# One f pair of each token pair by seven block products accumulated in the output's own banks, with double-width operand tiles, two weight slots and scattered due times

## The chip, the core and the metric

The kernel runs on one core of one Trainium2 chip. The metric is the device time of one execution in microseconds (us), the median of several runs. The kernel before takes 2160.39 us (three runs, 2159.62 to 2161.54). A core has five instruction streams that run side by side and wait for each other by semaphores: TensorE (PE, matrix products, with its weight loads PEld), VectorE (DVE), ScalarE (ACT), GpSimd (POOL), and SyncE (SP), which here issues the DMAs. On-chip tiles lie in SBUF; products are summed in eight PSUM banks of 128 x 512 numbers.

## The reference

Inputs are q, k, v of shape (4, 6080, 256), a scalar tau, w_in (256 x 2048) and w_out (2048 x 256), all 32-bit floats.

```python
qn = q / (norm(q, axis=1) + 1e-06);  kn = k / (norm(k, axis=1) + 1e-06)
s = kn.transpose(0, 2, 1) @ qn / tau          # 4 x 256 x 256
a = softmax(s, -1)
x = (v @ a).reshape(24320, 256)
h = x @ w_in                                  # 24320 x 2048
g = where(h >= 1, h, where(h <= -1, 0, (h + 1)**2 / 4))
out = g @ w_out                               # 24320 x 256
```

## The kernel before

The softmax of a batch is small, so the kernel first makes a matrix W = a @ w_in for each of the four batches and then computes h = v @ W, g, and g @ w_out. The last two products are nearly all of the work. Every product is made with three matmuls (`mm3`, line 473): each operand is split into a rounded first part and a rest (`hi` and `lo`), and first x first, first x rest, rest x first are summed. The three matmuls of one block are called a block product here.

A batch's 6080 tokens are cut into six token pairs (five of 2 x 512 tokens, the last of 2 x 480), and the 2048 hidden features into eight f pairs of 2 x 128. A token pair with an f pair is a group; there are 4 x 6 x 8 = 192 of them, numbered g. In each group:

- `h_ops` (line 801) makes the 2 x 2 blocks of h by `strassen` (line 642): seven block products instead of eight, in the banks A, B and Z. The banks serve as accumulators, and between products ScalarE copies a bank (lines 644, 646) and VectorE sums a bank and a copy (lines 649, 653).
- `tile_ops` (line 784) makes g of each of the four blocks: two ScalarE operations (saturate, line 790; square, 792), a VectorE maximum (794), and the split into a first part (796, ScalarE or VectorE, whichever the planner takes) and a rest (798, VectorE).
- `o_ops` (line 819) adds the group's share of the output into four banks, O00, O01, O10 and O11: eight block products. After the eighth f pair ScalarE copies the banks out (line 838) and SP stores them.

Meanwhile the Gram matrix and the softmax of the next batch are made (`gram_chunk`, `square_piece`, `softmax`), and seven sums of v's blocks for the next token pair (`make_V`, with four differences on GpSimd, line 746). The weights of a group (`w`, 896 KB with both parts) are made once a batch, stored in DRAM, and loaded again for each token pair (`load_W`) into one of four slots.

Nothing is run in the order in which it is written. Each operation is recorded with an engine, a planned duration, the buffers it reads and writes, and a due time (16 per group plus an offset). `Order.run` (line 125) then plays the program through: for each engine it takes, of the operations whose inputs are ready and whose pools have a free buffer, the one with the earliest due time, and so writes the engine's order. Pools marked `ordered` hand out buffers in the order in which they were asked for. A planned duration is a line in the number of columns; the planner knows a cost for a table load of ScalarE only as a longer first exponential (line 571), and none for two engines that disturb each other.

Of the kernel before, what the change touches and what calls it, by code (L numbers as in the profile page):

```python
# [58 lines left out]
class Order:  # L59
# [11 lines left out]
    def op(self, eng, dur, fn, r=(), w=(), due=0.0, gates=(), size=0, other=None, slack=0.0):  # L71
# [53 lines left out]
    def run(self):  # L125
# [3 lines left out]
        for o in self.ops:  # L129
            o.count = len(o.deps) + len(o.gates)  # L130
# [18 lines left out]
        while left:  # L149
            pick = None  # L150
            for e, ops in avail.items():
                now = free[e]
                best = None
                for o in ops:
                    t = base[o.n, e]
                    if best is not None and t > now + SOON and t >= best[0][0]:
                        continue
# [11 lines left out]
                    key = (now, o.due, o.n) if t <= now or o.due <= URGENT and t <= now + SOON else (t, o.due, o.n)  # L169
# [10 lines left out]
            for b in o.bufs:  # L180
                if b.ap is None:
# [44 lines left out]
U = 32  # L226
# [17 lines left out]
ET_SLACK = (2.0, 3.0)  # L244

# [10 lines left out]
def channel_attention_moe(ctx: ExitStack, tc: tile.TileContext, kq, kqT, vT, tau, w_in, w_out, outT):  # L256
# [42 lines left out]
    wout = sb("wout", [FP, 2, 2, C], F32R)  # L299

# [16 lines left out]
    u_mem = sb("u_mem", [6 * TB])  # L317
# [7 lines left out]
        "g": Pool([sb("g6", [2, TB], F32R), *[lambda j=j, h=h: slot2(j, h) for j in range(3) for h in range(2)]]),  # L325
        "w": Pool([w_mem[:, i * WSZ:(i + 1) * WSZ].rearrange("p (a j f) -> p a j f", a=2, j=NS) for i in range(4)]),
# [4 lines left out]
        "u": Pool([u_mem[:, i * TB:(i + 1) * TB] for i in range(6)]),  # L331
# [21 lines left out]
    pools["g"].held[1:] = [kq_all] * 6  # L353
# [10 lines left out]
    pools["u"].held[:4] = [u2_all] * 4  # L364
# [10 lines left out]
    def buf(pool):  # L375
        return Buf(pools[pool])
# [615 lines left out]
```

## Time and profile before

| | before |
|---|---|
| median of three timed runs | 2160.39 us (2159.62 to 2161.54) |
| profiled execution, span of its instructions | 2158.3 us |
| TensorE busy | 2147.2 us (99%), 9872 instructions |
| VectorE busy | 1783.1 us (83%) |
| ScalarE busy | 1593.0 us (74%) |
| GpSimd busy | 245.0 us (11%) |
| DMA, mean | 172 GB/s |

A busy time is the length of the span in which the engine ran at least one instruction. The span runs from the first instruction to the end of the last; the timed runs take in what lies around it. In the views, a group of instructions is told by its line, engine, operation and tiles (out<-in, buffer numbers left out), then its count, its busy time and the mean of one in ns, and the idle time of its engine ahead of it with what ended that idle time. Matmuls overlap, so the mean of one is longer than the distance from one to the next.

### The profile page before, as it was taken

How to read it: one execution, taken by the hardware profiler on the slowest of the kernel's cores; microseconds unless marked ns; L12 is line 12 of the kernel's file. 1: busy time of each engine (PE TensorE's matmuls, PEld its weight loads, DVE VectorE, ACT ScalarE, POOL GpSimd, SP SyncE). 2: the span in 40 equal slices, each digit the busy share in tenths (PEclk: the TensorE clock that was granted, in tenths of full speed). 3: DMA queues.
4: the chain of work that ended last, by engine and by line, in shares of the span. 5: the costliest groups of instructions: out<-in, count | busy, mean ns of one | idle time of the engine just before them, and what ended most of it. 6: DMA issues, size and time to landing. Idle time of an engine off the chain costs nothing.

```text
span 2158.3 us, 27952 instructions
## 1 busy us (share of the span) xinstructions
PE 2147.2 (99%) x9872; PEld 1802.1 (83%) x9872; DVE 1783.1 (83%) x2893; ACT 1593.0 (74%) x2818; POOL 245.0 (11%) x260
## 2 busy tenths in 40 slices
PE   9999999999999999999999999999999999999999
PEld 7888888888888888888888888888888888888887
DVE  7898888878798888888879888888787988777776
ACT  6687778777778777776778877777677777777776
POOL 0230020100131000000023000000012300001000
PEclk9999999999999999999999999999999999999999
DMA  9765366545665444544656455454556532332331
GB/s 385 299 225 172 130 205 206 174 164 156 202 222 181 172 158 163 202 156 133 198 174 234 173 183 172 154 192 140 138 201 202 173 124 91 132 126 94 121 120 36
DMA packets 124604, 371.46 MB, mean 172 GB/s; under 512 B 17968, under 2 KB 49584, under 8 KB 121904
## 3 DMA queue, kind: packets, MB, share of 16 engines
q1 hardware_dynamic: 124464, 369.67, 50.1%
q8 instruction: 78, 1.28, 0.2%
q14 instruction: 62, 0.51, 0.1%
HBM read 298.84 MB, written 70.78 MB: 171 GB/s over the span
## 4 chain that ended last, share of the span: by engine, by line
PE 96%; DMA 2%; DVE 1%; ACT 0%; POOL 0%; issue 0%; SPq 0%; ACTq 0%; DVEq 0%; POOLq 0%
PE bank L473 94%; PE bank L875 1%; DMA kq<-kq 1%; DMA raw_mem<-w_out 1%; DMA raw_mem<-vT 0%; DMA outT<-y_mem 0%; DVE mh_mem L891 0%; POOL t L746 0%; DVE u_mem L404 0%; ACT u_mem L790 0%; DVE w_mem L708 0%; ACT u_mem L792 0%; POOL cols L532 0%; DVE v L755 0%; DVE u_mem L401 0%
## 5 line engine op out<-in xcount | busy, mean ns | idle before, releaser
L473 PE MATMUL bank<-x,wout 128*128 128x512 f32 (+1 forms) x3948 | 1013.4, 388 | 0.0
L473 PEld LDWEIGHTS bank<-x,wout 128*128 128x128 f32 x3948 | 739.3, 188 | 147.0
L473 PE MATMUL bank<-v,w_mem 128*128 128x512 f32 (+1 forms) x3264 | 849.3, 388 | 1.1 <-ACT bank L646 0.6
L473 PEld LDWEIGHTS bank<-v,w_mem 128*128 128x128 f32 x3264 | 610.8, 188 | 122.9 <-ACT bank L646 1.2
L790 ACT ACTIVATE u_mem<-bank 128x512 f32<-128x512 f32 (+1 forms) x576 | 341.3, 593 | 252.9 <-PE bank L473 240.4
L794 DVE TENSOR_TENSOR u_mem<-bank,u_mem 128x512 f32<-128x512 f32 (+1 forms) x576 | 390.9, 680 | 131.3 <-ACT u_mem L792 130.2
L792 ACT ACTIVATE u_mem<-u_mem 128x512 f32<-128x512 f32 (+1 forms) x768 | 471.0, 626 | 6.8
L798 DVE TENSOR_TENSOR x<-u_mem,x 128x512 fp32r<-128x512 f32 (+1 forms) x658 | 457.1, 701 | 13.8 <-ACT x L796 8.7
L796 ACT CAST x<-u_mem 128x512 fp32r<-128x512 f32 (+1 forms) x300 | 183.9, 615 | 92.7 <-DVE u_mem L794 91.6
L649 DVE TENSOR_TENSOR bank<-bank,mh_mem 128x512 f32<-128x512 f32 (+1 forms) x198 | 137.2, 693 | 96.8 <-PE bank L473 93.0
L473 PE MATMUL bank<-x,w_mem 128*128 128x512 f32 (+1 forms) x768 | 208.8, 388 | 0.9 <-ACT bank L646 0.9
L473 PE MATMUL bank<-g,wout 128*128 128x512 f32 (+1 forms) x660 | 182.8, 387 | 0.0
L746 POOL TENSOR_TENSOR t<-raw_mem 128x512 f32<-128x512 f32 (+1 forms) x48 | 67.8, 1411 | 925.0 <-DMA raw_mem<-vT 542.7
L653 DVE TENSOR_TENSOR mh_mem<-bank,mh_mem 128x512 f32<-128x512 f32 (+1 forms) x198 | 135.6, 685 | 40.2 <-PE bank L473 35.2
L473 PEld LDWEIGHTS bank<-x,w_mem 128*128 128x128 f32 x768 | 143.6, 188 | 30.0 <-ACT bank L646 1.3
L797 DVE CAST x<-u_mem 128x512 fp32r<-128x512 f32 (+1 forms) x358 | 159.6, 452 | 8.0
L644 ACT COPY mh_mem<-bank 128x512 f32<-128x512 f32 (+1 forms) x198 | 115.3, 582 | 59.4 <-PE bank L473 57.3
L794 DVE TENSOR_TENSOR u_mem<-mh_mem,u_mem 128x512 f32<-128x512 f32 (+1 forms) x192 | 135.6, 706 | 13.6 <-ACT u_mem L792 13.3
L473 PEld LDWEIGHTS bank<-g,wout 128*128 128x128 f32 x660 | 123.7, 188 | 24.5
L646 ACT COPY bank<-bank 128x512 f32<-128x512 f32 (+1 forms) x198 | 113.4, 573 | 33.7 <-PE bank L473 28.0
L746 POOL TENSOR_TENSOR t<-raw_mem,t 128x512 f32<-128x512 f32 (+1 forms) x48 | 66.8, 1392 | 496.3 <-DVE v L755 394.1
L790 ACT ACTIVATE u_mem<-mh_mem 128x512 f32<-128x512 f32 (+1 forms) x192 | 118.9, 619 | 5.1 <-DVE mh_mem L653 3.7
(104 smaller groups left out, 1432.5 us busy)
## 6 DMA issues: line engine op xcount, KB each, us to landing
w_mem<-w_d SPq DMA_DIRECT2D x160, 896.0 KB, 4.6
raw_mem<-kqT SPq DMA_DIRECT2D x60, 512.0 KB, 6.2
w_d<-w_mem SPq DMA_DIRECT2D x32, 896.0 KB, 4.5
raw_mem<-kq SPq DMA_DIRECT2D x51, 512.0 KB, 5.5
kq<-kq SPq DMA_DIRECT2D x20, 1024.0 KB, 9.1
raw_mem<-vT SPq DMA_DIRECT2D x40, 512.0 KB, 6.3
outT<-y_mem SPq DMA_DIRECT2D x80, 256.0 KB, 2.8
win_mem<-wop_d SPq DMA_DIRECT2D x21, 512.0 KB, 5.6
```

Source lines behind the costliest of these rows:

```text
L473: nc.tensor.matmul(out, lhsT=lhs(a), rhs=rhs(c), start=start and m == 0, stop=stop and m == 2, skip_group_check=skip)
L644: op("ACT", act_us(n), lambda: nc.scalar.copy(m5.ap[:, :n], a.ap[:, :n]), r=[a], w=[m5], due=early)
L646: op("ACT", act_us(n), lambda: nc.scalar.copy(a.ap[:, :n], z.ap[:, :n]), r=[z], w=[a], due=early)
L649: op("DVE", dve_us(n), lambda: nc.vector.tensor_tensor(out=bb.ap[:, :n], in0=z.ap[:, :n], in1=m5.ap[:, :n], op=ALU.add), r=[z, m5], w=[bb] ...
L653: op("DVE", dve_us(n), lambda: nc.vector.tensor_tensor(out=h22.ap[:, :n], in0=z.ap[:, :n], in1=m5.ap[:, :n], op=ALU.add), r=[z, m5], w=[h2 ...
L746: op("POOL", pool_us(n), lambda: nc.gpsimd.tensor_tensor(out=tt(x), in0=a(), in1=c(), op=ALU.subtract), r=r, w=[ts[x]], due=due + d, gates ...
L790: op("ACT", act_us(n), lambda: nc.scalar.activation(us(), src(), IDENTITY_SAT240, scale=240.0), r=[h], w=[u], due=d_sat)
L792: op("ACT", act_us(n), lambda: nc.scalar.activation(us(), us(), AF.Square, bias=0.5, scale=1.0 / 480.0), w=[u], due=d_sq)
L794: op("DVE", dve_us(n), lambda: nc.vector.tensor_tensor(out=us(), in0=src(), in1=us(), op=ALU.max), r=[h], w=[u], due=d_max)
L796: op("ACT", act_us(n), lambda: nc.scalar.copy(t.ap[:, 0, :n], us()), r=[u], w=[t], due=d_hi, other=("DVE", dve1_us(n), lambda: nc.vector.t ...
L797: other=("DVE", dve1_us(n), lambda: nc.vector.tensor_copy(t.ap[:, 0, :n], us())) if g >= FIRST else None)
L798: op("DVE", dve_us(n), lambda: nc.vector.tensor_tensor(out=t.ap[:, 1, :n], in0=us(), in1=f32(t.ap[:, 0, :n]), op=ALU.subtract), r=[u], w=[ ...
```

## The change

In token pairs 2 to 6 of each batch (`SPLIT`), the first f pair's part of the output is made by seven block products. Four go into the four output banks directly. Three go into the bank O01 one after the other: after the first direct products ScalarE copies O01 and O11 aside, the bank takes one more product, VectorE adds the copy of O11 and keeps the sum, the bank takes the next product, ScalarE copies it, and then the last product. The other f pairs accumulate as before, and at the end VectorE adds the saved parts to three of the four banks. The operands are four differences of g blocks, made by GpSimd, and four sums of w_out blocks, made once.

Around it: tiles for g and its split hold two blocks each (`u` 5 x 1024, `g` 4 x 2 x 2 x 512 columns); the pool `w` has two slots instead of four; new pools `c` and `c2` hold the differences and copies; offsets of due times stand in two tables; in 30 of 96 stretches of due times a fixed pattern is added to each; the scratch for DMA descriptors is set to 1024. AHEAD is negative, so that the new branch in `run` takes nothing.

```diff
+            seed, width = NUDGE.get(max(0, int(o.due // (G * NUDGE_GROUPS))), (0, 0))
+            if seed and o.due > -100:
+                o.due += width * scatter(o.n, seed)
...
-U = 32
+U = 32.76
...
+SPLIT = ((0, 1, 1, 1, 1, 1), (0, 1, 1, 1, 1, 1), (0, 1, 1, 1, 1, 1), (0, 1, 1, 1, 1, 1))
+WN = 2
+T_STR = {
+    'sat00': 0.31,
...
-        "w": Pool([w_mem[:, i * WSZ:(i + 1) * WSZ].rearrange("p (a j f) -> p a j f", a=2, j=NS) for i in range(4)]),
+        "w": Pool([w_mem[:, i * WSZ:(i + 1) * WSZ].rearrange("p (a j f) -> p a j f", a=2, j=NS) for i in range(WN)], ordered=True),
...
+    def combos(g):
+        b, k, i = groups[g]
+        n = pairs[k][1]
+        d = G * g
+        u0, u1 = gu[g]
+        c2, c = sums[b, k, i] = buf("c2"), buf("c")
+        c2.parts, c.parts = [Buf(ap=()), Buf(ap=())], [Buf(ap=())]
+        for k_, out, o, a, x, c_, y in ((0, c2, 1, u1, 1, u1, 0), (1, u1, 0, u1, 0, u0, 0), (2, c2, 0, u1, 1, u1, 0),
+                                        (3, c, 0, u0, 1, c2, 0)):
+            op("POOL", pool_us(n), lambda out=out, o=o, a=a, x=x, c_=c_, y=y: nc.gpsimd.tensor_tensor(
+                out=half_of(out, o, n), in0=half_of(a, x, n), in1=half_of(c_, y, n), op=ALU.subtract),
+               r=[a.parts[x], c_.parts[y]], w=[out.parts[o]], h=[out, a, c_], due=d + T_STR["sum"][k_])
...
+    def strassen_o(g):
...
+        first = T_STR["direct"]
+        mm(o(0, 1), w_(i, 0, 0), wout_buf[i], gt[g, 0], 0, i == 0, d + first[0])
+        mm(o(1, 0), s_(i, 3), wsum_buf[i], gt[g, 1], 1, i == 0, d + first[1])
+        mm(o(1, 1), s_(i, 0), wsum_buf[i], gt[g, 1], 0, i == 0, d + first[2])
+        mm(o(0, 0), w_(i, 1, 0), wout_buf[i], gt[g, 0], 1, i == 0, d + first[3])
...
+        copy(z, (0, 0))
+        copy(o(1, 1), "m5")
+        late = lambda key, j: [(x, d + e + T_STR["late"] * (j - i)) for x, e in T_STR[key]]
+        t23 = [operand(sums[b, k, j][0], n, (late("hi2", j), late("lo2", j))) for j in range(SPLIT[b][k])]
+        for j in range(SPLIT[b][k]):
+            mm(z, s_(j, 1), wsum_buf[j], t23[j], 0, False, d + T_STR["chain"][0])
+        op("DVE", dve_us(n), lambda: nc.vector.tensor_tensor(out=r[1, 0].ap[:, :n], in0=z.ap[:, :n], in1=r["m5"].ap[:, :n],
+                                                            op=ALU.add), r=[z, r["m5"]], w=[r[1, 0]], due=early)
+        for j in range(SPLIT[b][k]):
+            mm(z, s_(j, 2), wsum_buf[j], t23[j], 1, False, d + T_STR["chain"][1])
+        copy(z, (1, 1))
+        for j in range(SPLIT[b][k]):
+            t = operand(sums[b, k, j][1], n, (late("hi4", j), late("lo4", j)))
+            mm(z, w_(j, 1, 1), wout_buf[j], t, 0, False, d + T_STR["chain"][2])
...
+                    r = sums.get((b, k), {}).get((y, ct))
+                    if r:
+                        op("DVE", dve_us(n), lambda o=o, yb=yb, r=r: nc.vector.tensor_tensor(
+                           out=yb.ap[:, :n], in0=o.ap[:, :n], in1=r.ap[:, :n], op=ALU.add), r=[o, r], w=[yb], due=due)
...
-                softmax(b + 1, d + 8)
+                softmax(b + 1, d + 19.26)
```

Two places of the built order. The first is TensorE's at the first f pair of the third token pair. Banks 0, 1, 6 and 7 are A, B and Z of h; banks 2 to 5 are O00, O01, O10 and O11; `wout` is w_out and `wsum` its sums. Before:

```order
L473 MATMUL bank4_112<-g6_94,wout_77 128x512 x3
L473 MATMUL bank5_113<-x1_703,wout_77 128x512 x3
L473 MATMUL bank7_115<-x3_1040,w_mem_85 128x512 x3
L473 MATMUL bank1_109<-x3_1040,w_mem_85 128x512 x3
L473 MATMUL bank5_113<-g6_94,wout_77 128x512 x3
L473 MATMUL bank7_115<-v0_95,w_mem_85 128x512 x3
L473 MATMUL bank0_108<-v4_99,w_mem_85 128x512 x3
L473 MATMUL bank2_110<-x0_675,wout_77 128x512 x3
L473 MATMUL bank6_114<-v5_100,w_mem_85 128x512 x3
L473 MATMUL bank2_110<-x2_752,wout_77 128x512 x3
L473 MATMUL bank3_111<-x0_675,wout_77 128x512 x3
L473 MATMUL bank3_111<-x2_752,wout_77 128x512 x3
```

and now:

```order
L575 MATMUL bank4_118<-x1_746,wsum_78 128x512 x3
L575 MATMUL bank3_117<-g0_95,wout_77 128x512 x3
L575 MATMUL bank7_121<-x3_1030,w_mem_86 128x512 x3
L575 MATMUL bank5_119<-x1_746,wsum_78 128x512 x3
L575 MATMUL bank2_116<-g0_95,wout_77 128x512 x3
L575 MATMUL bank1_115<-x3_1030,w_mem_86 128x512 x3
L575 MATMUL bank0_114<-v4_100,w_mem_86 128x512 x3
L575 MATMUL bank3_117<-x2_781,wsum_78 128x512 x3
L575 MATMUL bank7_121<-v0_96,w_mem_86 128x512 x3
L575 MATMUL bank6_120<-v5_101,w_mem_86 128x512 x3
L575 MATMUL bank2_116<-x1_746,wout_77 128x512 x3
L575 MATMUL bank3_117<-x2_781,wsum_78 128x512 x3
```

Before, the f pair has two rows for each of the four O banks (the first of bank 4 stands three rows above this piece). Now it has one row for each, and bank 3 takes two more here (with `wsum`) and a third 13 rows further down; the row of bank 2 with x1 belongs to the next f pair.

The second place is ScalarE's at the softmax of batch 2, in the last token pair of batch 1; the same rows stand at the softmax of batches 3 and 4. `sf_mem` holds the scores, so the rows that write it are the two exponentials. Before:

```order
L790 ACTIVATE u_mem_90<-bank7_115 128x512
L571 ACT_TABLE_LOAD
L571 ACTIVATE sf_mem_88,cols0_75<-sf_mem_88,cols0_75 128x256
L792 ACTIVATE u_mem_90<-u_mem_90 128x512
L571 ACTIVATE sf_mem_88,cols0_75<-sf_mem_88,cols0_75 128x256
L644 COPY mh_mem_86<-bank0_108 128x480
L796 CAST x2_752<-u_mem_90 128x512
L646 COPY bank0_108<-bank6_114 128x480
L796 CAST x2_752<-u_mem_90 128x512
L790 ACT_TABLE_LOAD
L790 ACTIVATE u_mem_90<-bank0_108 128x480
L792 ACTIVATE u_mem_90<-u_mem_90 128x480
```

and now (L673 is the exponential, L899 the saturation, L903 the square, L923 the cast):

```order
L673 ACT_TABLE_LOAD
L673 ACTIVATE sf_mem_89,cols0_75<-sf_mem_89,cols0_75 128x256
L899 ACT_TABLE_LOAD
L899 ACTIVATE u_mem_91<-bank0_114 128x480
L673 ACT_TABLE_LOAD
L673 ACTIVATE sf_mem_89,cols0_75<-sf_mem_89,cols0_75 128x256
L903 ACTIVATE u_mem_91<-u_mem_91 128x480
L899 ACT_TABLE_LOAD
L899 ACTIVATE u_mem_91<-mh_mem_87 128x480
L899 ACTIVATE u_mem_91<-bank1_115 128x480
L903 ACTIVATE u_mem_91<-u_mem_91 128x480
L923 CAST x2_781<-u_mem_91 128x480
```

A saturation has moved between the two exponentials, and two more table loads stand with it. Behind this piece follow a square, a saturation, `COPY mh_mem<-bank0`, a square and `COPY bank0<-bank7`; ahead of it stand `COPY bank0<-bank6` and three casts.

## Rows read from the trace of the kernel before

**Rows 1.** The page: busy us, share of the span and instructions of each engine

```profile
PE 2147.2 (99%) x9872; PEld 1802.1 (83%) x9872; DVE 1783.1 (83%) x2893; ACT 1593.0 (74%) x2818; POOL 245.0 (11%) x260
```

**Rows 2.** Windows: stretch, us, busy (instructions) of PE, PEld, DVE, ACT, POOL; PEclk, DMA

```profile
200.00:2150.00 1950.00, 1949.53 (x8951) 1636.33 (x8952) 1614.53 (x2648) 1450.33 (x2586) 209.40 (x215) 1.00 0.48 162
```

**Rows 3.** Waits of PE (us in total, times, longest), then the last on its timeline

```profile
PE bank L875 <- DMA kq<-kq: 3.0, 4, 1.7
PE bank L473 <- ACT bank L646: 1.5, 2, 0.9
...
200.47 0.96 PE L473 MATMUL bank<-x,w_mem 128*128 128x512 f32 x3 [0.91 <-ACT bank L646]
```

**Rows 4.** Timeline of PE: start us, us, instructions; at 170 and at 560 us

```profile
170.15 0.84 PE L473 MATMUL bank<-x,wout 128*128 128x512 f32 x3
170.83 0.84 PE L473 MATMUL bank<-g,wout 128*128 128x512 f32 x3
...
559.93 0.81 PE L473 MATMUL bank<-v,w_mem 128*128 128x480 f32 x3
560.58 1.46 PE L473 MATMUL bank<-x,wout 128*128 128x480 f32 x6
```

**Rows 5.** Groups by line and shape: busy us, mean ns | idle before

```profile
L790 ACT ACTIVATE u_mem<-bank 128x512 f32<-128x512 f32 x480 | 286.4, 597 | 212.2 <-PE bank L473 203.8
L796 ACT CAST x<-u_mem 128x512 fp32r<-128x512 f32 x255 | 157.3, 619 | 69.7 <-DVE u_mem L794 68.5
L798 DVE TENSOR_TENSOR x<-u_mem,x 128x512 fp32r<-128x512 f32 x549 | 385.2, 709 | 11.7 <-ACT x L796 7.6
L649 DVE TENSOR_TENSOR bank<-bank,mh_mem 128x512 f32<-128x512 f32 x166 | 115.9, 698 | 70.1 <-PE bank L473 69.3
L746 POOL TENSOR_TENSOR t<-raw_mem 128x512 f32<-128x512 f32 x40 | 57.4, 1436 | 712.2 <-DMA raw_mem<-vT 497.0 <-DVE mh_mem L653 97.0 <-DVE v L755 91.9
```

**Rows 6.** Timeline of ACT at the softmax of batch 2

```profile
510.06 1.28 ACT L571 ACT_TABLE_LOAD   x1
511.35 0.51 ACT L571 ACTIVATE sf_mem<-sf_mem,cols 128x256 f32<-128x256 f32 x1
511.77 0.18 ACT L571 ACTIVATION_READ_ACCUMULATOR sf_mem<-sf_mem,cols 128x1 f32 x1
...
513.32 0.62 ACT L796 CAST x<-u_mem 128x512 fp32r<-128x512 f32 x1
513.84 0.55 ACT L646 COPY bank<-bank 128x480 f32<-128x480 f32 x1
...
515.75 1.28 ACT L790 ACT_TABLE_LOAD   x1
517.04 0.57 ACT L790 ACTIVATE u_mem<-bank 128x480 f32<-128x480 f32 x1
517.65 0.60 ACT L792 ACTIVATE u_mem<-u_mem 128x480 f32<-128x480 f32 x1
```

**Rows 7.** Tile w_mem: the DMAs that load and store the weights' slots

```profile
DMA to landing us min/median/max: 3.5/4.6/13.5
```

**Rows 8.** SP's timeline from 488 us, and DMA issues there (KB, us to landing)

```profile
488.74 0.37 SPq L556 DMA_DIRECT2D rn_d<-cols  x1
490.39 0.32 SPq L379 DMA_DIRECT2D w_mem<-w_d  x1
...
w_mem<-w_d SPq DMA_DIRECT2D x2, 896.0 KB, 9.4
rn_d<-cols SPq DMA_DIRECT2D x1, 1.0 KB, 9.9
```

**Rows 9.** Timeline of DVE and of POOL at 301 to 305 us

```profile
300.71 0.69 DVE L798 TENSOR_TENSOR x<-u_mem,x 128x512 fp32r<-128x512 f32 x1
302.97 2.39 DVE L798 TENSOR_TENSOR x<-u_mem,x 128x512 fp32r<-128x512 f32 x2
...
303.01 1.80 POOL L746 TENSOR_TENSOR t<-raw_mem 128x512 f32<-128x512 f32 x1 [11.03 <-DVE x L797]
```

More of the change, by code (lines that the diff above doesn't have):

```diff
@@ L51 @@
 SOON = 0.3
+AHEAD, RATE = -21.03, 40.8
 class Op:
@@ L155, in run @@
                     t = base[o.n, e]
-                    if best is not None and t > now + SOON and t >= best[0][0]:
+                    if best is not None and t > now + max(SOON, AHEAD) and t >= best[0][0]:
                         continue
@@ L244, with scatter @@
 ET_SLACK = (2.0, 3.0)
+NUDGE_GROUPS = 2
+NUDGE = {
[4 rows of a table added]
+}
+def scatter(n, seed):
+    x = (n * 2654435761 + seed * 2246822519 + 374761393) & 0xFFFFFFFF
+    x ^= x >> 15
+    x = (x * 2246822519) & 0xFFFFFFFF
+    x ^= x >> 13
+    return x / 2**32 - 0.5
+SPLIT = ((0, 1, 1, 1, 1, 1), (0, 1, 1, 1, 1, 1), (0, 1, 1, 1, 1, 1), (0, 1, 1, 1, 1, 1))
+WN = 2
+T_PLAIN = {
+    'sat00': 6.19,
+    'sq00': 5.81,
+    'max00': 11.17,
+    'sat01': 14.41,
+    'sq01': -6.66,
+    'max01': 14.91,
+    'sat11': 17.12,
+    'sq11': 19.51,
+    'max11': 17.91,
+    'sat10': 19.72,
+    'sq10': 16.46,
+    'max10': 2.66,
+    'sq': 22.46,
+    'hi0': ((0, 14.67), (1, 22.07)),
+    'lo0': ((0, 19.38), (1, 26.54)),
+    'hi1': ((0, 20.12), (1, 21.1)),
+    'lo1': ((0, 19.91), (1, 21.44)),
+    'o': ((34.75, 36.49, 40.21, 37.06), (24.93, 26.82, 30.64, 29.37)),
+}
+T_STR = {
+    'sat00': 0.31,
+    'sq00': -6.27,
+    'max00': 12.71,
+    'sat01': 0.0,
+    'sq01': 9.23,
+    'max01': 36.97,
+    'sat11': 12.74,
+    'sq11': 18.89,
+    'max11': 26.25,
+    'sat10': 29.07,
+    'sq10': 17.32,
+    'max10': 7.81,
+    'sq': 47.08,
+    'hi0': ((0, -2.0), (1, 28.38)),
+    'lo0': ((0, 27.88), (1, 21.87)),
+    'hi1': ((0, 20.4), (1, 22.7)),
+    'lo1': ((0, 5.64), (1, 13.79)),
+    'sum': (30.04, 31.22, 27.0, 22.88),
+    'direct': (21.09, 27.49, 26.88, 27.74),
+    'chain': (30.85, 43.19, 53.35),
+    'hi2': ((0, 25.07), (1, 42.64)),
+    'lo2': ((0, 28.65), (1, 34.17)),
+    'hi4': ((0, 41.98),),
+    'lo4': ((0, 46.16),),
+    'late': -18.42,
+    'early': 5.9,
+}
 HEAD = (2,)
@@ new lines, in strassen_o, with mm, copy @@
+    def strassen_o(g):
+        b, k, i = groups[g]
+        t0, n = pairs[k]
+        d = G * g
+        w_ = lambda j, x, ct: (lambda a: wout[:, j, a, x, ct * P:(ct + 1) * P])
+        s_ = lambda j, m: (lambda a: wsum[:, j, a, m])
+        if i == 0:
+            for y in range(2):
+                for ct in range(CT):
+                    o_buf[b, k, y, ct] = buf(f"O{y}{ct}")
+        o = lambda y, ct: o_buf[b, k, y, ct]
+        def mm(out, lhs, wb, t, x, start, due):
+            op("PE", mm_us(n), lambda: mm3(out.ap[:, :n], lhs, lambda c: t.ap[:, c, x, :n], start, True),
+               r=[t.parts[x], wb], w=[out], h=[t], due=due)
+        first = T_STR["direct"]
[3 more added lines that the diff above has]
+        mm(o(0, 0), w_(i, 1, 0), wout_buf[i], gt[g, 0], 1, i == 0, d + first[3])
+        if i < SPLIT[b][k] - 1:
+            return
+        r = sums[b, k] = {x: buf("c") for x in ((0, 0), "m5", (1, 0), (1, 1))}
+        early = d + T_STR["early"]
+        z = o(0, 1)
+        def copy(src, x):
+            op("ACT", act_us(n), lambda: nc.scalar.copy(r[x].ap[:, :n], src.ap[:, :n]), r=[src], w=[r[x]], due=early)
+        copy(z, (0, 0))
[12 more added lines that the diff above has]
+            mm(z, w_(j, 1, 1), wout_buf[j], t, 0, False, d + T_STR["chain"][2])
```

172 lines of the change are left out of this document (120 added, 52 removed), and 4 rows, old and new, of the table NUDGE.

## The prediction

> **What bounds the kernel now.** I read the page's busy line first. TensorE works 99% of the span, VectorE 83%, ScalarE 74%, GpSimd 11% [rows 1]. An average could hide a stage with another limit, so the windows view came second. [...] Third, the waits of TensorE: 3.0 us for loads of kq lead the list, then 1.5 us in two waits for ScalarE's copy of a bank, and the later of these two, 0.91 us, is the last of all and ends at 200.47 us [rows 3]. So from 200 us on a matmul left out gives back its whole price, and a wait put in front of TensorE costs its whole length; work given to the other three engines costs nothing until TensorE waits for it. The profiled span is 2158.3 us, 2.1 us under the median of the timed runs (2160.4). I sum against the span and add 2.1 at the end.
>
> **What is removed.** In 5 of the 6 token pairs of each of the 4 batches the first f pair makes its output with 7 block products instead of 8. A block product is 3 matmuls, so 20 x 3 = 60 matmuls go; the built order agrees (9693 matmuls before, 9633 after). In 4 of the 5 token pairs a block has 512 columns, in the last 480. On the PE timeline three 512-column matmuls start 0.68 us after the three before them (170.15 to 170.83), three of 480 columns 0.65 us (559.93 to 560.58) [rows 4]. That is 16 x 0.68 + 4 x 0.65 = 13.5 us. The mean of 388 ns that the groups show for one matmul is no price: neighbours overlap.
>
> **What is added beside TensorE.** Each of the 20 places adds 4 GpSimd differences, 3 splits (a first part on ScalarE or VectorE, a rest on VectorE), 3 bank copies on ScalarE and one VectorE sum, and 3 of the 4 closing copies become VectorE sums. By the rows, VectorE gets 3 x 0.71 (rest) + 1 x 0.70 + 3 x 0.70 (sums) = 4.9 us, ScalarE up to 3 x 0.62 (the copies added and taken away are three each), GpSimd 4 x 1.44 = 5.8 us [rows 5]. Over 20 places that is about 98, 37 and 115 us. VectorE then stands near (1783 + 98) / 2145 = 88% and ScalarE near 77%: there is still room, and spreading it is the planner's work. The sums of w_out (4 small VectorE operations, a copy, a rest) come once, in the head. I take 0 for all this where the planner has placed it; what hides it is the free 17% and 26%, and if that cover fails, the price is that of the third rival.
>
> **What moves, and the one place where TensorE will wait.** Due times, U, the pools and the scatter move nothing but order. The order of ScalarE holds a change that the diff doesn't show. Before, the two exponentials of a batch's softmax stand with one square between them, one table load ahead and one behind. After, a saturation (which needs the other table) stands between them: the order has four table loads there instead of two, at each of the three changes of batch. The planner's cost for the second exponential (0.45) has no load in it. A load takes 1.28 us, and the next instruction starts when it ends (510.06 to 511.35) [rows 6].
>
> What that costs, worked out at that place. Start when TensorE has finished `bank6<-v6_102` and ScalarE may copy that bank (`bank0<-bank6`, the row before the three casts that precede the first table load). The clock of ScalarE, with pitches from the rows, which overlap by about 0.1 where nothing depends [rows 6]: copy 0.45 and three casts 0.52 each with a tail of 0.1 = 2.1; load 1.29, exponential with its read-out 0.60, load 1.29, saturation 0.57, load 1.29, exponential 0.60, square 0.61, load 1.29 = 7.5; then saturation, saturation, square, cast, square, saturation at 0.50, copy 0.45, square 0.50, copy 0.55 = 4.5. The last copy, bank7 into bank0, ends 14.1 us after the start. TensorE's `bank7<-v7_103` writes that bank and stands, in its own order, behind 33 matmuls of 512 and 21 of 480 columns: 33 x 0.227 + 21 x 0.217 = 12.0 us. So TensorE waits about 14.2 - 12.0 = 2.2 us, and nothing later gives it back. Without the two loads ScalarE would be there at 11.6 and TensorE would not wait. Three places: 6.6 us. I bound the term between 0 (ScalarE reaches the place 2.2 us early) and 5 us a place (it also arrives 2 to 3 us late from the heavier work before), that is 0 to 15 us.
>
> **The weights' slots.** `w` shrinks from 4 slots to 2. Counted in the order, between the last matmul that reads a slot and the first that reads its next content stood 123 to 345 matmuls; now 24 to 72, the middle one 42. At 0.227 us that is 5.4 to 16.3 us, middle 9.5. A load takes 4.6 us from issue to landing in the median, 13.5 at most [rows 7]. The longest ones are known: the store of 1 KB (`rn_d`) takes 9.9 us, and the load issued 1.7 us behind it is among two with a median of 9.4 [rows 8]. In the new order that load is released by TensorE some 32 matmuls (7.3 us) after the store and needed 74 matmuls (16.8 us) after it; 9.9 + 4.6 = 14.5, so it lands 2.3 us early. The smallest lead, 5.4 us against 4.6, holds as well. Behind the waiting load on SP's queue stand stores of outT and loads of raw, with leads of many us. I take 0.4 us for stray late ones; bounds 0 and 32 us (17 loads have 33 matmuls, 7.5 us, or fewer; each 1.9 us late if it took 9.4 like the pair in [rows 8]).
>
> **GpSimd beside VectorE.** The 80 new differences of 1.44 us run beside VectorE. The trace shows what that does: two VectorE rests that alone need 0.69 and, overlapped, 0.60 took 2.39 us while GpSimd's difference ran, 1.1 us more, and its own time rose from 1.44 to 1.80 [rows 9]. The planner has no such cost. But 96 differences of this kind and size run in the kernel now, and TensorE waits behind none of them after 201 us [rows 3]. The nearest row says 0; I take 0.4 us, and bound it at 80 x 1.1 = 88 us, and at 0 from below, since more GpSimd work can't speed the others.
>
> **Head and tail.** Up to matmul 230 the order has the same matmul count, and the waits there end with the same loads; I take 0, bounds -1 and +2 us. At the end a VectorE sum (0.70 [rows 5]) takes the place of a copy (0.55 [rows 6]) ahead of the last stores: 0.15, inside the rounding.
>
> **Sum.** 2158.3 - 13.5 + 6.6 + 0.4 + 0.4 = 2152.2 for the span, 2154.3 as timed. A measurement of this kernel can't tell less than 0.2% (4.3 us) from no change: faster means under 2156.1, slower over 2164.7.
>
> **The rivals.**
> First, the stall at the change of batch doesn't come (ScalarE runs ahead there; it waits 204 us for TensorE over the kernel in the saturation alone [rows 5]). Then 2154.3 - 6.6 = 2147.7. Against it: the four loads are instructions in the order, and the copies before them wait for TensorE, so ScalarE can't be early. Chance 0.14.
> Second, late weights: in the loads of W at the ends of batches (three stretches) and of the next softmax (three) the other loads hold a slot's load back by 1.5 us each: 2154.3 + 9 = 2163.3. For it: the largest landing of 13.5 [rows 7]. Against: SP issues those loads right behind the previous slot's, some 9 us before the next. Chance 0.10.
> Third, and on the other side, GpSimd's differences: where one of them holds VectorE back by 1.1 us just before a bank sum that TensorE waits for, TensorE stalls. It happens around the 20 places, with VectorE at 88%. At 0.08 us for each of the 80 on TensorE the gain that is left is gone, at 0.13 the kernel is slower by 0.2%; I price it at 0.18: 2154.3 - 0.4 + 14.4 = 2168.3. For it: the 1.1 us in [rows 9], and that a bank sum has only some 0.6 us to spare in the tightest spots of both orders (6 matmuls between, 1.36 us, less a sum of 0.70). Against it: no such stall in 1950 us. Chance 0.10.
> Fourth, a table load drags a drain behind it: after a load the exponential started 0.01 us after its end [rows 6], so nothing of the kind is seen, and I give it 0.02. [...]
> [...]
> That the kernel doesn't do what it says (the 60 matmuls come back elsewhere) is excluded by the count of the built order, up to 0.02.
>
> **How the numbers follow.** My forecast, 13.5 given and about 7 taken back at the three changes of batch, has 0.62 and its own range 2151 to 2158.5. Faster: three quarters of 0.62 and the first rival, 0.60. Slower: most of the third rival and half of the fourth, 0.09. Within 0.2%: the rest, 0.31. The range from 2146.5 to 2164.5 takes in the first and second rival; the third, the fourth and the worst of the bounds are outside.
>
> **What would show it.** Right: 9812 PE instructions on the page instead of 9872, six table loads of each kind at the change of batch, and in TensorE's waits three of about 2 us each for the ScalarE copy of bank7 (line 748), at about a quarter, a half and three quarters of the span; nothing else over 0.5 us after 200 us. Wrong: waits of TensorE for DMA w_mem (second rival); many waits for VectorE's bank sums (lines 751, 755, 1014) with rests longer than 1 us beside GpSimd (third); no wait at the changes of batch (first).

## The result, and the profile after

The changed kernel takes 2176.93 us (median of 4 runs, 2176.07 to 2177.21), the kernel before 2160.01 in the same rounds: 1.0075 times as long, 95% interval 1.0060 to 1.0089. The forecast was 2154.3, with a range up to 2164.5.

The page's busy line answers to [rows 1], the window from 200 to 2150 us to [rows 2]:

```profile
PE 2144.7 (99%) x9812; PEld 1785.8 (82%) x9812; DVE 1897.2 (87%) x2996; ACT 1653.3 (76%) x2927; POOL 365.5 (17%) x340
```

```profile
200.00:2150.00 1950.00, 1931.50 (x8816) 1606.43 (x8815) 1712.01 (x2722) 1494.87 (x2666) 323.39 (x291) 1.00 0.48 163
```

The 60 matmuls are gone. But TensorE, which stood idle for 0.5 us in this window before, stands idle for 18.5 us now, at the same granted clock of 1.00. Its waits (us in total, times, longest) answer to [rows 3]:

```profile
PE bank L575 <- DVE bank L751: 5.7, 7, 1.3
PE bank L575 <- ACT bank L748: 5.6, 4, 1.4
PE bank L575 <- DVE x L927: 3.9, 7, 0.9
...
PE bank L575 <- DMA w_mem<-w_d: 0.4, 1, 0.4
```

Before, no wait of TensorE for VectorE stood in the list's first rows; now a bank sum (L751) and the rests of the split (L927) are among the longest. A pause of TensorE cost a little more than itself here. Three matmuls of 480 columns start 0.65 us after the three before them [rows 4]; behind the pause below it is 0.77 (529.71 to 530.48). This is PE's timeline at the first change of batch (start, duration, instructions, the pause ahead of them and what ended it):

```profile
529.71 0.93 PE L575 MATMUL bank<-v,w_mem 128*128 128x480 f32 x3 [1.40 <-ACT bank L748]
530.48 0.82 PE L575 MATMUL bank<-x,w_mem 128*128 128x480 f32 x3
```

I added up by how much each matmul after 202 us starts later behind its neighbour than the median of its line and shape: 0.2 us before, 29.5 us now, in about 40 pauses with what follows them. 29.5 less the 13.5 us given is the 16.0 by which the span grew (2158.3 to 2174.3). By place, 14.1 of the 29.5 us stand within 12 us of the new differences at 16 of their 20 places (of the other four, one lies in the head and three at the changes of batch); 9.8 stand at the three changes of batch, and 5.6 beside GpSimd's differences for V, which the kernel before has too.

Where VectorE is late shows in one of the 20 places. First VectorE, then GpSimd, then TensorE:

```profile
1238.64 0.43 DVE L925 CAST x<-u_mem 128x512 fp32r<-128x512 f32 x1
1239.11 1.67 DVE L927 TENSOR_TENSOR x<-u_mem,x 128x512 fp32r<-128x512 f32 x1
1240.70 0.68 DVE L908 TENSOR_TENSOR u_mem<-bank,u_mem 128x512 f32<-128x512 f32 x1
1241.30 0.92 DVE L925 CAST x<-cc 128x512 fp32r<-128x512 f32 x1
1242.14 1.52 DVE L925 CAST g<-u_mem 128x512 fp32r<-128x512 f32 x1
1243.58 1.77 DVE L927 TENSOR_TENSOR x<-cc,x 128x512 fp32r<-128x512 f32 x1
1245.27 0.68 DVE L927 TENSOR_TENSOR g<-u_mem,g 128x512 fp32r<-128x512 f32 x1
```

```profile
1238.69 1.54 POOL L973 TENSOR_TENSOR cc<-u_mem 128x512 f32<-128x512 f32 x1 [17.22 <-DVE u_mem L908]
1240.31 1.63 POOL L973 TENSOR_TENSOR u_mem<-u_mem 128x512 f32<-128x512 f32 x1
1242.01 1.36 POOL L973 TENSOR_TENSOR cc<-u_mem 128x512 f32<-128x512 f32 x1
1243.45 1.35 POOL L973 TENSOR_TENSOR c<-u_mem,cc 128x512 f32<-128x512 f32 x1
```

```profile
1246.01 0.73 PE L575 MATMUL bank<-g,wout 128*128 128x512 f32 x2 [1.51 <-DVE g L927]
```

While GpSimd makes its four differences, a VectorE rest takes 1.67 and 1.77 us instead of 0.68, a cast 0.92 and 1.52 instead of 0.43. Both rests end 0.55 us behind the end of a difference, both casts 0.28 us, wherever in the difference they began. The first cast, begun just ahead of the first difference, keeps its 0.43, and the max at 1240.70, with a bank for one source, its 0.68. The rest at 1245.27, behind the last difference, is back at 0.68, but the two rests and two casts before it have gathered 3.7 us of delay (0.99 + 0.49 + 1.09 + 1.09), and TensorE waits 1.51 us for it. So in these rows the rests, with two sources in SBUF, are held up until a difference ends (1.67 and 1.77 us), the casts, with one, likewise, but for the first (0.92 and 1.52), and the max, with a bank for the other source, is not (0.68). What holds them up the rows don't show.

### The profile page after: what moved, and what is told of

It reads as the page before. It is cut to its first block, busy times and chain, and to the rows that moved or that the text cites. A ratio compares the mean times of both kernels' runs of the same rounds, so it can differ in the third digit from the quotient of the medians.

```text
span 2174.3 us, 28156 instructions
## 1 busy us (share of the span) xinstructions
PE 2144.7 (99%) x9812; PEld 1785.8 (82%) x9812; DVE 1897.2 (87%) x2996; ACT 1653.3 (76%) x2927; POOL 365.5 (17%) x340
## 4 chain that ended last, share of the span: by engine, by line
PE 86%; DVE 7%; DMA 3%; ACT 2%; issue 1%; POOL 0%; SPq 0%; ACTq 0%; POOLq 0%; DVEq 0%
PE bank L575 84%; DVE x L927 2%; PE bank L1087 1%; DVE u_mem L908 1%; DMA raw_mem<-vT 1%; DVE x L925 1%; DMA kq<-kq 1%; DVE g L927 1%; DMA raw_mem<-w_out 1%; DVE bank L751 1%; DVE y_mem L1047 0%; ACT u_mem L899 0%; ACT L673 0%; POOL t L848 0%; DVE mh_mem L1103 0%
## 5 line engine op out<-in xcount | busy, mean ns | idle before, releaser
L575 PE MATMUL bank<-x,wout 128*128 128x512 f32 (+1 forms) x3198 | 814.3, 388 | 1.9 <-DVE x L927 1.9
L575 PEld LDWEIGHTS bank<-v,w_mem 128*128 128x128 f32 x3240 | 603.9, 188 | 141.2 <-DVE bank L751 8.5
L575 PEld LDWEIGHTS bank<-x,wout 128*128 128x128 f32 x3198 | 598.6, 188 | 123.2 <-DVE x L927 4.2
L899 ACT ACTIVATE u_mem<-bank 128x512 f32<-128x512 f32 (+1 forms) x576 | 341.0, 593 | 225.9 <-PE bank L575 219.8
L903 ACT ACTIVATE u_mem<-u_mem 128x512 f32<-128x512 f32 (+1 forms) x768 | 470.3, 626 | 6.0
L908 DVE TENSOR_TENSOR u_mem<-bank,u_mem 128x512 f32<-128x512 f32 (+1 forms) x576 | 388.9, 678 | 55.9 <-ACT u_mem L903 54.4
L927 DVE TENSOR_TENSOR x<-u_mem,x 128x512 fp32r<-128x512 f32 (+1 forms) x570 | 414.3, 735 | 12.5 <-ACT x L923 7.9
L575 PE MATMUL bank<-g,wout 128*128 128x512 f32 (+1 forms) x1110 | 283.9, 388 | 1.7 <-DVE g L927 1.7
L575 PEld LDWEIGHTS bank<-g,wout 128*128 128x128 f32 x1110 | 207.7, 188 | 43.8 <-DVE g L927 2.6
L923 ACT CAST x<-u_mem 128x512 fp32r<-128x512 f32 (+1 forms) x302 | 183.4, 614 | 64.2 <-DVE u_mem L908 62.2
L575 PE MATMUL bank<-x,w_mem 128*128 128x512 f32 (+1 forms) x792 | 218.7, 389 | 2.3 <-ACT bank L748 1.4
L751 DVE TENSOR_TENSOR bank<-bank,mh_mem 128x512 f32<-128x512 f32 (+1 forms) x198 | 136.8, 691 | 74.1 <-PE bank L575 72.5
L755 DVE TENSOR_TENSOR mh_mem<-bank,mh_mem 128x512 f32<-128x512 f32 (+1 forms) x198 | 135.3, 683 | 39.8 <-PE bank L575 36.3
L927 DVE TENSOR_TENSOR g<-u_mem,g 128x512 fp32r<-128x512 f32 (+1 forms) x198 | 149.1, 757 | 4.4 <-ACT g L923 3.1
L908 DVE TENSOR_TENSOR u_mem<-mh_mem,u_mem 128x512 f32<-128x512 f32 (+1 forms) x192 | 133.1, 693 | 13.5 <-ACT u_mem L903 12.9
L925 DVE CAST x<-u_mem 128x512 fp32r<-128x512 f32 (+1 forms) x268 | 132.2, 497 | 5.2
L748 ACT COPY bank<-bank 128x512 f32<-128x512 f32 (+1 forms) x198 | 113.8, 575 | 27.1 <-PE bank L575 21.6
```

Source lines behind the costliest of these rows:

```text
L575: nc.tensor.matmul(out, lhsT=lhs(a), rhs=rhs(c), start=start and m == 0, stop=stop and m == 2, skip_group_check=skip)
L748: op("ACT", act_us(n), lambda: nc.scalar.copy(a.ap[:, :n], z.ap[:, :n]), r=[z], w=[a], due=early)
L751: op("DVE", dve_us(n), lambda: nc.vector.tensor_tensor(out=bb.ap[:, :n], in0=z.ap[:, :n], in1=m5.ap[:, :n], op=ALU.add), r=[z, m5], w=[bb] ...
L755: op("DVE", dve_us(n), lambda: nc.vector.tensor_tensor(out=h22.ap[:, :n], in0=z.ap[:, :n], in1=m5.ap[:, :n], op=ALU.add), r=[z, m5], w=[h2 ...
L899: op("ACT", act_us(n), lambda: nc.scalar.activation(half_of(u, x, n), h.ap[:, :n], IDENTITY_SAT240, scale=240.0), r=[h], w=[u.parts[x]], h ...
L903: op("ACT", act_us(n * (1 + (x is None))), lambda: nc.scalar.activation(part_of(u, x, n), part_of(u, x, n), AF.Square, bias=0.5, scale=1.0 ...
```

## The experiments

All were timed in 5 rounds against the kernel before (2160.5 to 2161.0 us); a time has the 95% interval of its ratio to before behind it. Theory: GpSimd's differences slow VectorE just where it has no room, and the four table loads add the rest. Rivals: the amount of the added work; the new due times, scatter and pools; the wait for the differences' results.

**Small differences.** Instructions, orders and waits as in the changed kernel; GpSimd's 80 differences do 8 columns.

```
-  out=half_of(out, o, n), in0=half_of(a, x, n), in1=half_of(c_, y, n)
+  out=half_of(out, o, 8), in0=half_of(a, x, 8), in1=half_of(c_, y, 8)
```

> The changed kernel with GpSimd's 80 differences on 8 of their 512 columns, the rest of the tiles set to zero at the start (so f2, f3 and f4's operands are not computed); every instruction stays in its place in every engine's order, and every wait too. Theory (GpSimd's differences hold VectorE's SBUF work back, and VectorE comes late to the banks that TensorE waits for): most of the roughly 20 us of short stalls outside the batch changes go, 2158 to 2166 us. Rival A (VectorE and ScalarE are late from the added casts, remainders and sums themselves): 2174 to 2177 us. Rival B (the order from the new due times is what makes them late): the same, 2174 to 2177 us.

Measured: 2160.06 us, 0.9998 times before (0.9989 to 1.0007). 16.9 us came back (the same number as the kernel's whole loss by coincidence). VectorE is 39.8 us less busy with the same instructions:

```profile
PE 2137.6 (99%) x9812; PEld 1788.2 (83%) x9812; DVE 1857.4 (86%) x2996; ACT 1651.9 (77%) x2927; POOL 272.8 (13%) x345
```

So the differences' size costs 16.9 us, 0.21 each; the order and VectorE's own added work stayed. Not quite all of it need be theirs: of the 16.7 us between the two profiled executions, 1.1 are there at 91 us already, ahead of the first difference (186 us). The place agrees: of the late starts, the 14.1 us at the 16 places are gone whole, while 8.3 us stay at the changes of batch and 7.0 beside V's differences.

**Differences on VectorE.** `nc.gpsimd` becomes `nc.vector` in the same line; the other engines keep their order.

> The changed kernel with the same 80 differences done by VectorE, each at the place in VectorE's order where it stood in the order of all engines; nothing else moves. [...] Rival A (VectorE is late from the amount of its work): 55 us more of it at 87% load, 2190 us or more.

I had estimated 2172 to 2182 us: 80 x 0.69 = 55 us come to VectorE, what it loses beside each difference goes (0.49 to 1.09 us an operation in the rows above), and the two about cancel.

Measured: 2172.46 us (1.0044 to 1.0070 times before), 4.5 less than the changed kernel. VectorE does 80 operations more (3076 for 2996) and is busy as long:

```profile
PE 2145.6 (99%) x9812; PEld 1786.9 (82%) x9812; DVE 1896.3 (87%) x3076; ACT 1653.3 (76%) x2927; POOL 244.1 (11%) x260
```

Work given to GpSimd took as much of VectorE's time as doing it there; it was no relief. The 2190 us of rival A fall with this.

**Nothing split.**

```
-SPLIT = ((0, 1, 1, 1, 1, 1), (0, 1, 1, 1, 1, 1), (0, 1, 1, 1, 1, 1), (0, 1, 1, 1, 1, 1))
+SPLIT = ((0,) * 6,) * 4
```

> The changed kernel with no pair done by seven products (all 96 output stretches by eight), and the new pools, two weight slots, new due times and scatter kept; the order is planned anew. TensorE has its 60 matmuls (13.5 us) back, VectorE and GpSimd lose the added work. Theory (about 20 of the lost 29.5 us come from the added work beside GpSimd's differences, 9 from the batch changes): 2176.9 + 13.5 - 20 = about 2170, between 2163 and 2174 us. Rival B (the new due times, scatter, pools and weight slots lose the time): 13.5 us above the changed kernel, 2185 us or more.

Measured: 2181.07 us (1.0079 to 1.0110). My number was 11 too low, the rival's 2185 was 4 too high: in an order planned with the new due times, two weight slots and scatter, but without the work they were set for, 20.5 us are lost against before. Among TensorE's waits:

```profile
PE bank L574 <- DMA w_mem<-w_d: 6.2, 2, 4.5
...
PE bank L574 <- DVE x L926: 2.2, 4, 0.6
PE bank L574 <- DVE bank L750: 1.5, 6, 0.4
```

It is another order than the changed kernel's, so the 20.5 us are no share of that one's loss; they show what an order does by itself.

**Exponentials side by side**, the saturation ahead of both, two table loads fewer at each change of batch; the other engines keep their order.

```
-  lambda it=it: nc.scalar.activation(
-      sv(it), sv(it), AF.Exp, bias=nmax()[:, it:it + 1], accum_out=sums()[:, it:it + 1]),
+  lambda it=it: [nc.scalar.activation(
+      sv(i), sv(i), AF.Exp, bias=nmax()[:, i:i + 1], accum_out=sums()[:, i:i + 1])
+      for i in (((), range(CT))[it] if b else (it,))],
```

> The changed kernel with one thing moved: the first exponential of each later batch's softmax is emitted right before the second, so the saturation that stood between them goes ahead of both, and two table loads of ScalarE fall away at each of three batch changes; the order on every other engine is unchanged. Theory (the split exponentials make ScalarE about 2.5 to 3 us late there, and TensorE waits for its bank copy): 3 times 2.5 to 3.1 us less than the changed kernel's 2176.9, so 2167.5 to 2169.5 us. Rival (the stall at the batch change comes from the softmax's other work or from DMA): within 2 us of 2176.9.

Measured: 2172.78 us (1.0046 to 1.0071), 4.1 less, half of what I expected.

**No table loads at all**: in later batches `AF.Square` stands for `AF.Exp`.

> The changed kernel with squares in the place of the exponentials of batches 2 to 4 (so their softmax is not computed), which need no table of their own: all four table loads at each of the three batch changes fall away, and nothing else moves. Theory (ScalarE is late at the batch changes by its table loads): the stalls of about 3.1 us at each go whole, 8 to 9.5 us less than 2176.9, 2167 to 2169 us; the kernel with the exponentials side by side, which kept two loads, took 4.1 us off. Rival (the loads are half of it, the rest is the softmax's other work and its DMAs): 2171.5 to 2174 us.

Measured: 2171.37 us (1.0033 to 1.0061), 5.6 less, the rival's side. ScalarE runs 12 instructions fewer (2915 for 2927), the loads. Waits for L748 fell from 5.6 to 1.3 us (the one left stands at 91 us, in the head), but those for weight loads rose from 0.4 to 3.4: with ScalarE in time, another was late.

```profile
PE bank L575 <- DMA w_mem<-w_d: 3.4, 3, 1.3
...
PE bank L575 <- ACT bank L748: 1.3, 1, 1.3
```

**Unread work.** Is it contention, or the wait for the differences' results? On top of the small differences GpSimd got 100 subtractions of 384 columns that nobody reads: five behind the fourth difference of a place; or one behind each and two behind the fourth; or so placed with two different constant sources instead of one scratch tile. The diff is the first; the second has `1 + (out is c)` for the count, the third also two parts of `wout` for `in0` and `in1`.

```
   op=ALU.subtract),
+  *(nc.gpsimd.tensor_tensor(out=scr, in0=scr, in1=scr, op=ALU.subtract)
+    for _ in range(5 * (out is c)))
```

> The kernel small_differences (2160.1 us) with GpSimd given its work back on a tile that nobody reads: behind the fourth small difference of each of the 20 stretches stand five subtractions of 384 columns in place on a scratch tile (1920 columns, beside the 4 x 512 = 2048 of the changed kernel); f2, f3 and f4's operands are still not computed, and every other engine keeps its order. Theory (GpSimd's work beside VectorE's loses the time by itself): most of the 16.9 us come back, 2169 to 2178 us. Rival (it was the wait for the differences' results that lost the time): 2159 to 2163 us.

> As unrelated_work (2167.7 us: the unread subtractions behind the fourth difference of a stretch), but with one of them right behind each small difference and two behind the fourth, so that GpSimd's work stands where the changed kernel has it. Theory (GpSimd's work beside VectorE's loses the time, and its place decides how much): 2172 to 2178 us, as the changed kernel. Rival (what the displaced work did not bring back was the wait for the differences' results): 2166 to 2169 us, as before.

> As unrelated_in_place (2162.6 us), with the unread subtractions of 384 columns taking two different constant tiles for sources, as the differences do, where they had one scratch tile for both and took 0.82 us (the differences take 1.53). Theory (VectorE loses time beside GpSimd, and in unrelated_in_place it lost only half, 1878.3 us busy against 1857.4 with small differences and 1897.2 in the changed kernel): VectorE busy 1890 us or more, and 2168 to 2178 us. Rival (the wait for the differences' results is the rest): VectorE busy as high, and still 2160 to 2166 us. If VectorE's busy time stays near 1878 us, the run tells nothing.

Measured: 2167.69 us (1.0020 to 1.0043), 2162.62 us (1.0002 to 1.0019) and 2171.43 us (1.0036 to 1.0063). The first fell 1.3 us short of my range, and the second missed: I had expected the changed kernel's time. But VectorE had lost only half as much there. The three busy lines, in this order:

```profile
PE 2142.0 (99%) x9812; PEld 1786.6 (83%) x9812; DVE 1884.6 (87%) x2996; ACT 1653.2 (76%) x2927; POOL 379.9 (18%) x446
```

```profile
PE 2140.9 (99%) x9812; PEld 1788.2 (83%) x9812; DVE 1878.3 (87%) x2996; ACT 1652.5 (76%) x2927; POOL 374.9 (17%) x446
```

```profile
PE 2144.7 (99%) x9812; PEld 1786.3 (82%) x9812; DVE 1892.3 (87%) x2996; ACT 1653.6 (76%) x2927; POOL 396.2 (18%) x446
```

VectorE busy 1857.4, 1878.3, 1884.6, 1892.3 us goes with 2160.1, 2162.6, 2167.7, 2171.4, and the changed kernel's 1897.2 with 2176.9. Work that no one waits for brings 11.4 of the 16.9 us. The other 5.5 are not told apart: VectorE loses 4.9 us more in the changed kernel, and ScalarE waits there 4.9 us in all for the differences' results.

**The kernel before with unread work**: one subtraction of 512 columns behind each max of the 20 places; the other engines keep their order.

```
-  lambda: nc.vector.tensor_tensor(out=us(), in0=src(), in1=us(), op=ALU.max)
+  lambda: [nc.vector.tensor_tensor(out=us(), in0=src(), in1=us(), op=ALU.max),
+           *(nc.gpsimd.tensor_tensor(out=scr, in0=scr, in1=scr, op=ALU.subtract)
+             for _ in range(groups[g][1] > 0 and groups[g][2] == 0))]
```

> The kernel before with 80 GpSimd subtractions of 512 columns on a scratch tile that nobody reads, one behind each of the four max operations of the 20 stretches in which the changed kernel has its differences; every other engine keeps its order. Theory: VectorE loses about 0.5 us beside each (46 us over the 80 in the changed kernel), and what of it reaches TensorE depends on how much room the order leaves: 3 to 17 us above 2160.6. Rival (the kernel before has the room that the changed kernel's 98 more VectorE operations took): within 3 us of 2160.6.

This kernel also sets the scratch for DMA descriptors to 1024, as in the changed kernel.

Measured: 2188.70 us, 1.0130 times before (1.0116 to 1.0144): 27.7 us, 0.35 for each of the 80, beyond my range. VectorE goes from 1783.1 to 1827.2 us. TensorE's waits:

```profile
PE bank L473 <- DVE mh_mem L653: 9.0, 9, 2.0
...
PE bank L473 <- DVE x L799: 3.3, 3, 1.1
PE bank L473 <- DVE u_mem L794: 2.2, 5, 0.7
```

Contention, with not one instruction added to TensorE, VectorE or ScalarE, makes VectorE late for TensorE, in an order that had no such wait. The scratch was not tried by itself, but behind the head TensorE waits for no DMA in this run.

**The same computation in other orders.** If place decides, an order that knows the contention should win. The planner was told that a difference and a VectorE operation between SBUF tiles keep one another out for a share of their durations, and the two exponentials became one step. At first only that, with due times chosen by the planner's own end time. (The expectation says no scatter, but this kernel scatters 36 stretches of due times.)

```
+  t = max(base[o.n, e], lock) if o.lk and e in ("DVE", "POOL") else base[o.n, e]
...
+  lock = t + HF * o.dur if o.lk and o.eng in ("DVE", "POOL") else lock
```

> The changed kernel with its planner told that a GpSimd difference and a VectorE operation between SBUF tiles hold one another up (each is taken to block the other for half of its duration), the two exponentials in one step, no scatter, and due times chosen anew by the planner's own end time with that rule; the work is the changed kernel's. Theory: the differences then stand where VectorE has bank work or room, and 8 to 20 us of the 29.5 us of stalls go: 2157 to 2169 us. Rival (an order cannot avoid it, VectorE at 87% is always in GpSimd's way): 2172 us or more.

Measured: 2171.04 us (1.0033 to 1.0060): 5.9 better, but 2 us above my range and 1 under the rival's. Then two with scatter and due times chosen by replaying the planned order with measured durations, the two exponentials again one step; the planner's share of the durations is 0.8 in a. The replay is an estimate: at each difference it keeps VectorE's operations between SBUF tiles back for 1.1 us, the amount of [rows 9]. It gives 29 us of stalls for the changed kernel, where the trace has 29.5, 26 for the exponentials side by side, where it has 26.3, and 2 to 4 for a.

> [...] Theory (the stalls come from differences that stand where VectorE has no room, so an order can take them away): 5 to 12 us of stalls stay, 2152 to 2159 us, below both kernels. Rival (the work itself is too much for VectorE, or the replay leaves out what matters): 2165 us or more, as for the order planned with the cruder rule (2171.0).

> As replanned_a, with 0.65 for the share of the durations and another set of due times found in the same way (2 to 4 us of stalls in the replay). Theory: 2152 to 2159 us. Rival: 2165 us or more.

Measured: 2157.29 us (0.9975 to 0.9992 times before) and 2167.86 us (1.0021 to 1.0045). The second missed by 9: the replay hadn't seen late weights. They are what stayed in both, 11.5 us of waits in b and one in a. SP's issues in a, the store's landing time there, and the windows around the pause of TensorE that follows:

```profile
1011.79 0.38 SPq L662 DMA_DIRECT2D rn_d<-cols  x1
1014.57 0.32 SPq L466 DMA_DIRECT2D w_mem<-w_d  x1
```

```profile
rn_d<-cols SPq DMA_DIRECT2D x1, 1.0 KB, 9.9
```

```profile
1015.00:1022.00 7.00, 7.00 (x32) 5.79 (x32) 5.27 (x10) 4.17 (x8) 0.00 (x0) 1.00 0.82 38
1022.60:1026.00 3.40, 0.09 (x1) 0.00 (x0) 0.53 (x1) 1.20 (x3) 0.00 (x0) 0.95 0.75 221
1026.40:1032.40 6.00, 6.00 (x14) 4.72 (x15) 2.11 (x5) 2.20 (x5) 0.00 (x0) 0.50 0.35 103
1033.00:1040.00 7.00, 7.00 (x32) 5.79 (x31) 6.66 (x12) 4.72 (x10) 1.54 (x1) 1.00 0.02 7
```

The load issued 2.8 us behind the 1 KB store (9.9 us, as in [rows 8]) came 3.67 us late, and after that pause TensorE's granted clock was 0.50 for 6 us, with 14 matmuls in it; the 7 us of the first row hold 32. So the planner got one rule more: that store keeps the queue for 6 us.

```
-  size=P * 128, slack=RN_SLACK[0])
+  size=RN_SLACK[0] * 430e3, slack=0.5)
```

> As replanned_a (2157.3 us), with one rule more in the planner: the store of the row norms keeps the DMA queue for 6 us, so that a weight load is not planned right behind it with two weight slots only; 0.7 for the share of the durations, due times found anew in the replay (2 to 4 us of stalls). Theory (what was left in replanned_a was the late weight load of 3.8 us and the slower matmuls behind it): 2149 to 2154 us. Rival (other stalls take its place): 2156 us or more.

> As replanned_c with 0.8 for the share and other due times (2 to 3 us of stalls in the replay). Theory: 2149 to 2154 us. Rival: 2156 us or more.

Measured: 2154.31 us for d (0.9959 to 0.9982 times before; 0.3 above my range), and 2149.80 us for c (2148.15 to 2152.52), 0.9952 times before (0.9940 to 0.9965): the fastest version, 10.7 us under before and 27.1 under the changed kernel. Its page and the longest of its waits after the head:

```profile
PE 2134.9 (99%) x9812; PEld 1789.6 (83%) x9812; DVE 1830.2 (85%) x2914; ACT 1677.1 (78%) x3003; POOL 366.9 (17%) x340
```

```profile
PE bank L579 <- ACT bank L752: 2.3, 3, 1.2
...
PE bank L579 <- DVE kqs L589: 1.1, 1, 1.1
```

GpSimd works as long as in the changed kernel, and VectorE is 67 us less busy. Its rests and casts of one shape (busy us, mean ns), in the changed kernel and then in this one:

```profile
L927 DVE TENSOR_TENSOR x<-u_mem,x 128x512 fp32r<-128x512 f32 x476 | 348.7, 740 | 10.4 <-ACT x L923 6.4
...
L925 DVE CAST x<-u_mem 128x512 fp32r<-128x512 f32 x225 | 112.3, 503 | 4.1
```

```profile
L931 DVE TENSOR_TENSOR x<-u_mem,x 128x512 fp32r<-128x512 f32 x476 | 339.4, 722 | 10.7 <-ACT x L927 8.7
...
L929 DVE CAST x<-u_mem 128x512 fp32r<-128x512 f32 x182 | 78.2, 435 | 4.0 <-PE bank L579 0.9
```

They run shorter (722 for 740, 435 for 503), as they did with small differences (710 and 461), and VectorE has 82 instructions fewer, ScalarE 76 more: casts went over to the engine with room. What each of the two gave was not tried.

## Why the prediction was wrong

- **What is removed** (13.5 us): right. 9812 matmuls, and the balance of the span needs the 13.5.
- **What is added beside TensorE** (0): GpSimd's amount was right (+120.5 us, forecast 115). VectorE's 87% (forecast 88) is right by luck: the planner gave casts to ScalarE, so VectorE got 103 instructions more and not some 140, and with small differences it stands only 74 us above before (forecast 98); contention made up the rest. ScalarE got +60 where I had 37 (which makes 76%, not the 77 of the forecast). The step "I take 0 for all this where the planner has placed it" rested on a planner that doesn't know what GpSimd does to VectorE.
- **The table loads** (6.6 us): right in place and about right in size. TensorE waits 1.40 us, not 2.2, for L748 at 529.7 us and likewise at 1064 and 1601. ScalarE's last copy ended 14.05 us after the start, as worked out (14.1); TensorE came there 0.7 us later than worked out, having waited for VectorE on the way. Without any loads 5.6 us came back. No run shows the drain of the fourth rival: in the changed kernel, too, an exponential starts 0.01 us after its load has ended (517.75 + 1.28 us, then 519.04).
- **The weights' slots** (0.4 us): right in this order, one wait of 0.4. The lead is thin, though: the orders of replanned_a, replanned_b and no_split ran into the mechanism I had named, with 3.7 to 11.5 us.
- **GpSimd beside VectorE** (0.4 us): this is the step that failed; 16.9 us. The price per operation was there (1.1 us in [rows 9]); the argument "96 differences of this kind and size run in the kernel now, and TensorE waits behind none of them" took rows from another order and other places for these. Before's differences prepare V pairs ahead of their use, and even they cost TensorE something in the new order (last point). The new ones stand where VectorE serves TensorE's banks, and as before_with_work shows, such work costs 0.35 us apiece there even in before's order. The third rival had the mechanism, the rows (bank sums L751 and L755 late, rests over 1 us beside GpSimd) and almost the price: 0.18 us for each difference against 0.21. Its 0.10 should have been the largest share: at 88% load the room before a bank sum was known to be 0.6 us, less than the 1.1 of one collision.
- **Head and tail** (0): right. Matmul 230 starts at 57.75 us, before at 57.69; from the end of the last matmul to the end of the span it is 3.9 us, before 3.8.
- **The sum.** Before's 2160.0 - 13.5 + 16.9 + 5.6 gives 2169.0; 7.9 us are open. They are no single thing that a run took away: with small differences TensorE still waits 5.4 us for VectorE (L751, L908, L927), beside V's own differences and at the changes of batch, each pause costs about 0.1 us more behind it, and whether the 16.9 and 5.6 simply add was not tried. By place, the late starts that the two experiments leave are those beside V's differences (5.6 us; before's order has none) and 4.2 of the 9.8 us at the changes of batch, 9.8 us in all. (That is more than 7.9 because 1.9 of the 16.9 lie in the head: 1.1 ahead of the differences and 0.8 at their first place.) At one place of V's the trace shows how it comes about (first GpSimd, VectorE, then TensorE):

```profile
399.51 1.60 POOL L848 TENSOR_TENSOR t<-raw_mem 128x512 f32<-128x512 f32 x1 [1.03 <-DVE x L857]
399.89 1.77 DVE L927 TENSOR_TENSOR x<-u_mem,x 128x512 fp32r<-128x512 f32 x1
...
404.31 0.69 DVE L751 TENSOR_TENSOR bank<-bank,mh_mem 128x512 f32<-128x512 f32 x1
...
405.06 1.20 PE L575 MATMUL bank<-v,w_mem 128*128 128x512 f32 x4 [1.32 <-DVE bank L751]
```

A rest beside V's difference ends 1.09 us late, VectorE is free for at most 0.04 us at a time from there to the end of the bank sum, and TensorE waits 1.32 us for the bank sum. So the kind of work that was harmless before costs time in the new order too. No run made V's differences smaller, so their share is read from the trace and not tested. That the due times and scatter hold a part of the 7.9 is likely from no_split, not shown.

What the forecast said of the work was attainable: the same products take 2149.8 us in another order (with two table loads fewer at each change of batch). It was wrong in trusting this order with it.

## What to carry to other kernels

Work moved to GpSimd wasn't free for VectorE here: count its SBUF work at what it takes from VectorE (0.5 us a difference, 39.8 us for 80, near the 0.69 that a subtraction of VectorE takes [rows 9]), and ask what TensorE waits for behind it. That similar operations run harmlessly elsewhere in the kernel says nothing of a new place, unless the room there is the same. An order written by a planner is as good as its costs: when a change adds a kind of overlap the planner has no cost for, price the overlap from the trace at the tightest place, not at the mean.

## What the runs showed of the hardware

- With other operands GpSimd's work took more of VectorE's time: 100 unread subtractions of 384 columns took 0.82 to 1.34 us, 0.83 in the median, with one tile for both sources and made VectorE 20.9 us busier (1878.3 for 1857.4); at the same places with two tiles they took 1.16 us in the mean and made it 34.9 us busier (1892.3).
- After a pause of 3.67 us in replanned_a TensorE's granted clock was 0.50 for the next 6 us; in the 6 us behind the changed kernel's pauses of 1.40 and 1.51 us (529.71, 1064.07, 1246.01 and 1600.57 us) it was 1.00.
- Behind the short pauses of the changed kernel the following matmuls stood about 0.1 us further apart than usual: 0.77 us for 0.65 behind the pause of 1.40 at 529.71, 0.80 for 0.68 behind that of 1.19 at 1515.09.
